# Moving a tile's load and split, and the weights' loads, to later places in the attention stage of a fused attention and two-layer MLP

## The chip, the cores and the metric

The kernel runs on one core of one Trainium2 chip. The metric is the device time of one execution in microseconds; the time before is 1116.73 us, the median of 3 runs (1113.96 to 1124.78).

## The reference

Three parts follow each other. The whole is float32 in and out.

```python
# attention: batch 4, 8 heads, 576 positions, head dimension 64
scores = q @ k.T / 8 + bias          # bias: a small MLP of the relative position, per head
attn = exp(scores - max(scores)); attn = attn / (sum(attn) + 1e-9)
x = (attn @ v) as [2304 tokens, 512]
# layer 0: w_in [512, 2048], w_out [2048, 512]
h = x @ w_in;  x = (h * cos(h)) @ w_out
# layer 1: the same sizes, h = max(h, 0) + alpha * min(h, 0) in the place of h * cos(h)
```

The four weight matrices arrive as 64-bit floats, and are made into 32-bit ones on the chip.

## The kernel before, in words

**Attention** works on 16 pairs n (four pairs of heads, each for four batches; n = 4 * head pair + batch). A pair has five stages s: stages 1 to 4 hold 128 query rows of both heads, stage 0 the last 64 rows of both. A stage is: TensorE computes S (`emit_S`, L457), VectorE adds the bias and takes the maximum (`emit_max`, L473, tile P, or Pr for stage 0), ScalarE takes the exponential in place (`emit_exp`, L486). Then TensorE turns P (L550, L561, into T), ScalarE and VectorE copy that out of PSUM (L535, L537), and TensorE multiplies by v (L572, L575). Each pair's output goes to the DRAM tensor x_d in two pieces, A and B (L593). Pairs 0 to 3 are begun while the bias is still computed; from pair 4 (`FIRST`) on, TensorE's order is fixed, and the order of stages in a pair is 1, 0, 2, 3, 4.

**Weight jobs** run beside the attention, one step at a time (`step`, `bg`). A job `wi(0, f)` prepares one of 16 slabs of layer 0's w_in: SyncE loads the raw 64-bit slab into a tile raw (`load_raw`, two buffers), ScalarE makes two integer parts of it (wc L217 and wp L218, in `conv`), VectorE does two operations on wc (L223, L224), GpSimd adds wp (L227), then splits it into a rounded high and a low part (L306, L310), so that two TensorE products of reduced precision make one of float32. Slabs 6 to 15 are staged in a tile st and stored to w_d (L313). A job `stage_wo(0, k)` for k = 3 to 7 takes two slabs of w_out, raw 2k and 2k + 1, combines them, and splits four groups one after another through the same single-buffered tile st, then named sw: high part on ScalarE (L243), low part on GpSimd (L245), one or two stores to DRAM (L260). The next group's high part has to wait for these stores.

**Layer 0** (`h_phase0`) begins with the first tile of x, the first 512 tokens, which are batch 0: its four pieces xlo0 to xlo3 come from pairs 0, 4, 8 and 12. For each piece `split_x` loads xlo from x_d on SyncE's queue (L185), and splits it: xhi on ScalarE (L768), the low part on GpSimd (L770). These are written late in the program, but a scheduler (with a timeline of its own, and priorities) sets each engine's order, and puts an operation with few conditions early; ScalarE, VectorE, GpSimd and SyncE then take their lists strictly in that order. `behind` adds a condition to the scheduler's order: with its default kind it puts one instruction after another without a wait at run time.

In h_phase0, TensorE computes h (L785), ScalarE, VectorE, ScalarE and VectorE compute h * cos(h) (L793 to L798), and the rest of the weight jobs runs beside it.

Of the kernel before, what the change touches and what calls it, by code (L numbers as in the profile page):

```python
# [9 lines left out]
F32 = mybir.dt.float32  # L10
F32R = mybir.dt.float32r
I32 = mybir.dt.int32
U32 = mybir.dt.uint32
I64 = mybir.dt.int64
AF = mybir.ActivationFunctionType
# [25 lines left out]
FIRST, SIDE, SMOD, BFIRST, BRATE, SPL, WS0, WSR, PER = 4, 6, 2, 8, 2.5, 3, 28, 3.2, 1.0  # L41
# [30 lines left out]
def attn_mlp_kernel(ctx: ExitStack, tc: tile.TileContext, a: dict, out: bass.AP):  # L72
    nc = tc.nc
    ve, se, ge, te, sy = nc.vector, nc.scalar, nc.gpsimd, nc.tensor, nc.sync
# [94 lines left out]
    keep = lambda k, ins: tc.keep_in_program_order(ins) if k < len(KEEP) and KEEP[k] else ins  # L169
# [9 lines left out]
    raws_w = {}  # L179
    pinned = []  # L180
    anchor = []
    last = [None]

    def fetch(out, in_):
# [2 lines left out]
    def behind(ins, prev, kind=mybir.DependencyClass.NoSync):  # L187
        tc.add_manual_dep(ins.ins, prev.ins.name, mybir.DependencyInfo(kind, mybir.DependencyReason.DATA), reason="order")
        return ins

    def later(ins, prev):
        return behind(ins, prev, mybir.DependencyClass.Sync)

    def load_raw(layer, f, part):
        src = (a["wi1"], a["wi2"])[layer][f] if part == 0 else (a["wo1"], a["wo2"])[layer][f * 128:(f + 1) * 128, :]
        nm = f"{layer}_{f}_{part}"
        if wide:
            raw = wpool["s"].tile([128, 512, 2], I32, tag="raw", name=f"raw{nm}")
            ins = fetch(raw.rearrange("p n t -> p (n t)"), src.bitcast(I32))
        else:  # L200
            raw = wpool["s"].tile([128, 512], F32, tag="raw", name=f"raw{nm}")
            ins = fetch(raw, src)
        if anchor:
            behind(ins, anchor[-1])
        raws_w[layer, f, part] = raw

    def conv(layer, f, part, box):
        nm = f"{layer}_{f}_{part}"
        if (layer, f, part) not in raws_w:
            load_raw(layer, f, part)  # L210
            yield
        raw = raws_w.pop((layer, f, part))
        signed = layer == 1 and part == 1
        if wide:
            c = wpool["c"].tile([128, 512], I32, tag="c", name=f"wc{nm}")
            p = wpool["c"].tile([128, 512], I32, tag="p", bufs=1, name=f"wp{nm}")
            se.activation(out=c.bitcast(F32), in_=raw[:, :, 1].bitcast(F32), func=AF.Copy, scale=2.0 ** -112)  # L217
            se.activation(out=p, in_=raw[:, :, 0].bitcast(U32), func=AF.Copy, scale=2.0 ** -29)  # L218
            yield
            if signed:  # L220
                ve.tensor_scalar(c, c, 3, zs[:, f:f + 1].bitcast(I32), op0=ALU.logical_shift_left, op1=ALU.bitwise_xor)
            else:
                ve.tensor_scalar(c, c, 3, None, op0=ALU.logical_shift_left)  # L223
            ve.scalar_tensor_tensor(out=c, in0=raw[:, :, 1], scalar=-2 ** 31, in1=c,  # L224
                                    op0=ALU.bitwise_and, op1=ALU.bitwise_xor)
            yield
            ge.tensor_tensor(out=c, in0=c, in1=p, op=ALU.add)  # L227
            yield
            box.append(c.bitcast(F32))
        else:  # L230
            if signed:
                ve.tensor_scalar(raw, raw, sgn[:, f:f + 1], None, op0=ALU.mult)
                yield
            box.append(raw)
# [83 lines left out]
    bg = []  # L318

    def step(n=1):  # L320
        for _ in range(n):
            if not bg:
                return
            g = bg.pop(0)
            try:
                with tc.high_priority(offset=LP):
                    next(g)
            except StopIteration:
                continue
            bg.insert(0, g)  # L330

    def attention():
        with ExitStack() as c:
# [41 lines left out]
            sums = {}  # L375
# [105 lines left out]
            def emit_exp(n, s, h, e, nm):  # L481
                u, col = place[s, h]
                if (n, u) not in sums:
                    count["m"] += 1
                    sums[n, u] = sume[count["m"] % len(sume)]
                keep(3, se.activation(out=e, in_=e, func=AF.Exp, bias=nm, scale=-1.0,  # L486
                                      accum_out=sums[n, u][:, col, 0:1]))
                Pt[n, s, h] = e


# [179 lines left out]
            ns = 0  # L670
            NS = len(stages)
            i = j = 0
            while i < NS or pend_exp or waiting or fill:
                new = []
                if i < NS:
                    n, u, s = stages[i]
                    if n == FIRST:
                        steady.append(1)
                    hp, b = pairs[n]
                    more_bias(max(BFIRST + int(BRATE * j), GNEED[s]))  # L680
                    for m in range(FIRST, NP):
                        f = pos[m, 1]
                        if i == f - 6:
                            load_qkv(m)
                            splits[m] = split_qk(m)
                        if f - SPL <= i < f:
                            next(splits[m], None)
                    while n not in done:
                        next(side, None)
                    pss = emit_S(n, s)  # L690
                    new = [(n, s, h) + emit_max(n, s, h, ps) for h, ps in enumerate(pss)]
                for x in range(len(pend_exp) if i >= NS else len(pend_exp) + len(new) - ELAG):
                    if not pend_exp:
                        pend_exp, new = new, []
                    emit_exp(*pend_exp.pop(0))
                pend_exp += new
                if i < NS:
                    if b == B - 1 and hp + 1 < NHP:
                        for h in range(len(pss)):
                            load_bias(hp + 1, s + 4 * h)  # L700
                    if ng == NG and ns < len(JOBS) and j >= WS0 + WSR * due:
                        make, args, cost, need = JOBS[ns]
                        if ns == 0:
                            load_raw(*need[0])
                        bg.append(make(*args))
                        if ns + 1 < len(JOBS):
                            load_raw(*JOBS[ns + 1][3][0])
                        due += cost
                        ns += 1
                while waiting and all((waiting[0][0], *k) in Pt for k in place if place[k][0] == waiting[0][1]):  # L710
                    recip(*waiting[0])
                    fill += fillers(*waiting.pop(0))
                m = 2 if s else 1
                credit += PER * (1.85 if s else 1.6)
                if steady:
                    if i >= NS and not pend_exp and not waiting:
                        fill += tails.pop() if tails else []
                    want = {1: (0, 1), 0: (0, 3), 2: (0, 2), 3: (0, 1, 3), 4: (0, 2)}[s] if i < NS else range(4)
                    while fill and fill[0][2] in want:
                        fill.pop(0)[1]()  # L720
                else:
                    while fill and credit > 0:
                        d, fn, _ = fill.pop(0)
                        credit -= d
                        fn()
                    if not fill:
                        credit = min(credit, 0.0)
                wsteps += SR * m
                step(int(wsteps))
                wsteps -= int(wsteps)  # L730
                j += m
                i += 1
# [9 lines left out]
    def h_phase0():  # L742
# [5 lines left out]
        with ExitStack() as c:  # L748
# [7 lines left out]
            def split_x(t, cc):  # L756
                t0, n = TILES[t]
                xp = (wpool["x"], xh_p, xs_p, wpool["x"], xh_p)[t]
                width = 256 if t == 2 else TMAX
                lo = xp.tile([128, width], F32R, tag="xlo", name=f"xlo{t}_{cc}")  # L760
                r = lo.bitcast(F32)
                ins = fetch(r[:, 0:n], x_d[cc, :, t0:t0 + n])
                if anchor:
                    behind(ins, anchor[-1])
                yield
                hi = xp.tile([128, width], F32R, tag="xhi", name=f"xhi{t}_{cc}")
                xt[t, cc] = (hi, lo)
                se.activation(out=hi[:, 0:n], in_=r[:, 0:n], func=AF.Copy)  # L768
                eng = ve if t else ge
                eng.tensor_tensor(out=lo[:, 0:n], in0=r[:, 0:n], in1=hi[:, 0:n].bitcast(F32), op=ALU.subtract)  # L770
                yield
# [447 lines left out]
```

## Time and profile before

| | us |
|---|---|
| median of 3 runs | 1116.73 |
| the profiled execution | 1119.18 |
| its span, first to last instruction | 1117.4 |
| TensorE (PE) busy | 1063.2 |
| VectorE (DVE) busy | 809.9 |
| ScalarE (ACT) busy | 646.0 |
| GpSimd (POOL) busy | 255.0 |

A row of a view names the line, the engine, the operation and the tiles (out<-in). Idle time stands in brackets behind the operation that ended it, with what released it. Matmuls overlap, and their ends are modelled, so the idle time of PE is read more safely than its busy time. The steady attention is read here by pairs: the stretch from one pair's first exponential to the next one's.

### The profile page before, as it was taken

The page shows a single profiled execution, that of the slowest core. Times are in us where ns is not written, and L with a number is a line of the kernel's source. Part 1 is how long each engine was busy: PE and PEld are TensorE (multiplying, and loading weights), DVE is VectorE, ACT ScalarE, POOL GpSimd, SP SyncE. Part 2 cuts the span into 40 slices and gives each one's busy share as a digit, 9 for nine tenths or more (in the row PEclk, how much of TensorE's full clock was granted, in tenths as well). Part 3 has the DMA queues.
Part 4 walks back from the last instruction along what each step waited for, and adds up shares of the span by engine and source line. Part 5 has one row for each costly group of instructions (what it writes and reads, how often), then busy time and mean ns, then how long its engine had stood idle before and what let it go on. Part 6 is the DMA issues. An engine that isn't in the chain of part 4 may idle for free.

```text
span 1117.4 us, 18861 instructions
## 1 busy us (share of the span) xinstructions
PE 1063.2 (95%) x7078; PEld 900.6 (81%) x7078; DVE 809.9 (72%) x1304; ACT 646.0 (58%) x1084; POOL 255.0 (23%) x248
## 2 busy tenths in 40 slices
PE   7689899999799998999899999999999999999998
PEld 2246577777567787988799999998888889999998
DVE  8886687767775789787677777757766747767673
ACT  6897678867775565565344454456555534444442
POOL 5305666655442120000000000312322210000000
PEclk9899999999999999999999999999999999999999
DMA  8666657756449773535657455596666549654621
GB/s 274 215 179 184 200 154 225 231 163 231 158 148 316 266 253 132 161 131 170 216 199 228 149 159 181 201 333 211 215 217 206 199 152 346 209 199 128 212 66 49
DMA packets 107660, 219.77 MB, mean 197 GB/s; under 512 B 11569, under 2 KB 57393, under 8 KB 106161
## 3 DMA queue, kind: packets, MB, share of 16 engines
q1 hardware_dynamic: 77104, 157.74, 44.4%
q10 hardware_dynamic: 28032, 50.34, 12.0%
q0 software_dynamic: 2432, 10.49, 2.4%
q8 instruction: 56, 0.92, 0.4%
q14 instruction: 36, 0.29, 0.1%
HBM read 133.98 MB, written 84.56 MB: 196 GB/s over the span
## 4 chain that ended last, share of the span: by engine, by line
PE 71%; DMA 8%; DVE 6%; ACT 3%; issue 2%; POOL 1%; SPq 0%; ACTq 0%; POOLq 0%; DVEq 0%
PE v L1114 18%; PE ob L983 14%; PE h L785 9%; PE oc L983 9%; PE oa L983 9%; PE S L457 4%; DMA w_d<-sw 3%; PE x_B L575 2%; PE T_B L550 2%; PE T_A L550 1%; DVE tb L794 1%; POOL sw L245 1%; PE x_A L575 1%; DVE tb L795 1%; DVE tb L798 1%
## 5 line engine op out<-in xcount | busy, mean ns | idle before, releaser
L1114 PE MATMUL v<-x,v 128*128 128x512 f32 (+1 forms) x984 | 198.0, 364 | 0.0
L785 PE MATMUL h<-xhi,w 128*128 128x512 f32 (+1 forms) x640 | 186.0, 374 | 7.8 <-DVE tb L798 7.6
L1114 PEld LDWEIGHTS v<-x,v 128*128 128x128 f32 x984 | 168.5, 189 | 29.5
L785 PEld LDWEIGHTS h<-xhi,w 128*128 128x128 f32 x640 | 116.8, 190 | 31.4 <-issue 7.9
L227 POOL TENSOR_TENSOR wc<-wc,wp 128x512 int32<-128x512 int32 x64 | 85.6, 1337 | 208.8 <-DVE wc L224 151.8
L785 PE MATMUL h<-xlo,w 128*128 128x512 f32 (+1 forms) x320 | 119.3, 373 | 0.0
L965 ACT ACTIVATE op<-a 128x768 fp32r<-128x768 f32 x84 | 70.5, 844 | 83.5 <-PE ob L983 27.3
L966 DVE TENSOR_TENSOR op<-a,op 128x768 fp32r<-128x768 f32 x84 | 80.1, 957 | 51.0 <-ACT op L965 50.0
L473 DVE CUSTOM_DVE_ANT_0 P<-S,bt 128x576 f32<-128x576 f32 x128 | 91.5, 750 | 29.1 <-PE S L457 19.3
L486 ACT ACTIVATE P<-P,nm 128x576 f32<-128x576 f32 x128 | 98.5, 772 | 19.3 <-DVE nm L473 19.1
L965 ACT ACTIVATE op<-b 128x768 fp32r<-128x768 f32 x84 | 70.7, 844 | 65.6 <-PE ob L983 23.4
L966 DVE TENSOR_TENSOR op<-b,op 128x768 fp32r<-128x768 f32 x84 | 79.7, 954 | 30.0 <-ACT op L965 29.9
L1125 DVE SCALAR_TENSOR_TENSOR u<-v,asg,u 128x1024 f32<-128x1024 f32 (+2 forms) x48 | 48.0, 1013 | 40.5 <-ACT u L1124 40.1
L983 PE MATMUL ob<-op,wo 128*128 128x384 f32 x432 | 76.4, 336 | 0.0
L983 PEld LDWEIGHTS ob<-op,wo 128*128 128x128 f32 x432 | 75.1, 188 | 0.0
L793 ACT ACTIVATE ta<-h,quart 128x1024 int32<-128x1024 f32 (+1 forms) x40 | 40.9, 1023 | 51.7 <-PE h L785 31.1
L785 PEld LDWEIGHTS h<-xlo,w 128*128 128x128 f32 x320 | 60.8, 190 | 11.0
L457 PE MATMUL S<-kh,qh 64*128 64x288 f32 (+1 forms) x270 | 54.4, 355 | 15.1 <-DVE nm L473 14.2
L1124 ACT ACTIVATE u<-v,sgn 128x1024 f32<-128x1024 f32 (+2 forms) x48 | 43.0, 898 | 40.7 <-PE v L1114 40.6
L794 DVE SCALAR_TENSOR_TENSOR tb<-ta,h 128x1024 f32<-128x1024 int32 (+1 forms) x40 | 44.4, 1109 | 24.5 <-ACT ta L793 24.4
L797 ACT ACTIVATE tb<-tb,hpi 128x1024 f32<-128x1024 f32 (+1 forms) x40 | 42.3, 1059 | 24.6 <-DVE tb L795 17.1
L224 DVE SCALAR_TENSOR_TENSOR wc<-raw,wc 128x512 int32<-128x512 int32 x64 | 54.0, 848 | 1.3
(154 smaller groups left out, 2148.1 us busy)
## 6 DMA issues: line engine op xcount, KB each, us to landing
a<-g_d SPq DMA_DIRECT2D x60, 384.0 KB, 4.5
b<-g_d SPq DMA_DIRECT2D x48, 384.0 KB, 5.0
raw<-in_wi_dram SPq DMA_DIRECT2D x32, 512.0 KB, 3.8
raw<-in_wo_dram SPq DMA_DIRECT2D x32, 512.0 KB, 4.1
g_d<-tb ACTq DMA_DIRECT2D x32, 512.0 KB, 3.4
g_d<-u ACTq DMA_DIRECT2D x28, 512.0 KB, 2.9
bias_d<-be SPq DMA_DIRECT2D x36, 295.5 KB, 3.6
w_d<-sw SPq DMA_DIRECT2D x35, 256.0 KB, 3.1
```

Of the source, the lines that this page charges most:

```text
L224: ve.scalar_tensor_tensor(out=c, in0=raw[:, :, 1], scalar=-2 ** 31, in1=c, op0=ALU.bitwise_and, op1=ALU.bitwise_xor)
L227: ge.tensor_tensor(out=c, in0=c, in1=p, op=ALU.add)
L457: pe(te.matmul(ps[:, hf, 0:HS], lhsT=w[r, 128 * i:128 * i + 128], rhs=m[r, c0:c0 + HS], start=(j == 0), stop=(j == len(terms) - 1)))
L473: keep(2, ve.tensor_tensor_reduce(out=sn.rearrange("p (a b) -> p a b", a=2), in0=ps[:, :, 0:HS], in1=bt[hp, s].rearrange("p (a b) -> p a b ...
L486: keep(3, se.activation(out=e, in_=e, func=AF.Exp, bias=nm, scale=-1.0, accum_out=sums[n, u][:, col, 0:1]))
L785: te.matmul(ps, lhsT=w_[:, wx, w], rhs=xx[:, 0:n], start=(j == 0), stop=(j == 11))
L794: ve.scalar_tensor_tensor(out=g, in0=tt, scalar=-C1, in1=h, op0=ALU.mult, op1=ALU.add)
L965: se.activation(out=o[:, 0], in_=x, func=AF.Copy)
L966: lows.append(ve.tensor_tensor(out=o[:, 1], in0=x, in1=o[:, 0].bitcast(F32), op=ALU.subtract))
L983: ins = te.matmul(ps[:, m], lhsT=x[:, sl] if L else w[:, sl], rhs=w if L else x, start=first, stop=kk == NK - 1 and n == 2, skip_group_che ...
L1114: ins = te.matmul(both[:, i, 0:a1 - a0], lhsT=w[:, wx, 128 * cc:128 * cc + 128], rhs=x[:, xx, cc, a0 - o:a1 - o], start=(n == 0), stop=(n ...
L1125: ve.scalar_tensor_tensor(out=g, in0=ps, scalar=asg[:, f:f + 1], in1=g, op0=ALU.mult, op1=ALU.max)
```

## The change

Four edits, none of which adds or removes an operation; one of SyncE's issues becomes a merged row. (1) The load of the first x tile's piece cc is put behind the first exponential of pair 4cc + 2, and its high part behind the first exponential of pair 4cc + 3. (2) The loads of a job's raw slabs come in the order of their use: a job `stage_wo` first asks for its own second slab, and the next job's first slab is asked for after that. (3) From pair 4 to the end of the attention, raw loads and the two ScalarE parts of `conv` are put behind the exponential that was written last. (4) Exponentials lose their own program-order mark, which was off before (`KEEP` has two entries).

```diff
+    def hold(ins):
+        return behind(ins, exps[-1]) if FIRST in firsts and not pinned else ins
...
         if anchor:
             behind(ins, anchor[-1])
+        hold(ins)
         raws_w[layer, f, part] = raw
...
-            se.activation(out=c.bitcast(F32), in_=raw[:, :, 1].bitcast(F32), func=AF.Copy, scale=2.0 ** -112)
-            se.activation(out=p, in_=raw[:, :, 0].bitcast(U32), func=AF.Copy, scale=2.0 ** -29)
+            hold(se.activation(out=c.bitcast(F32), in_=raw[:, :, 1].bitcast(F32), func=AF.Copy, scale=2.0 ** -112))
+            hold(se.activation(out=p, in_=raw[:, :, 0].bitcast(U32), func=AF.Copy, scale=2.0 ** -29))
...
+    def job(g, more, nxt):
+        for r in more:
+            load_raw(*r)
+        k = 0
+        for _ in g:
+            if nxt and k >= (2 if more else 0):
+                load_raw(*nxt)
+                nxt = None
+            yield
+            k += 1
...
-                keep(3, se.activation(out=e, in_=e, func=AF.Exp, bias=nm, scale=-1.0,
-                                      accum_out=sums[n, u][:, col, 0:1]))
+                exps.append(se.activation(out=e, in_=e, func=AF.Exp, bias=nm, scale=-1.0,
+                                          accum_out=sums[n, u][:, col, 0:1]))
+                firsts.setdefault(n, exps[-1])
...
-                        bg.append(make(*args))
-                        if ns + 1 < len(JOBS):
-                            load_raw(*JOBS[ns + 1][3][0])
+                        bg.append(job(make(*args), need[1:], JOBS[ns + 1][3][0] if ns + 1 < len(JOBS) else None))
...
                 ins = fetch(r[:, 0:n], x_d[cc, :, t0:t0 + n])
-                if anchor:
-                    behind(ins, anchor[-1])
+                behind(ins, anchor[-1] if anchor else firsts[4 * cc + 2])
...
-                se.activation(out=hi[:, 0:n], in_=r[:, 0:n], func=AF.Copy)
+                ins = se.activation(out=hi[:, 0:n], in_=r[:, 0:n], func=AF.Copy)
+                if not t:
+                    behind(ins, firsts[4 * cc + 3])
```

What the scheduler makes of it: TensorE's order is the same row for row. The other four engines differ in the attention and a little in h_phase0. The conv of job f comes up to one job later than before, and has caught up by the time of `raw0_6_1`, w_out's first slab. Piece 0 of x stays where it was on both queues; piece 1's high part moves by a pair, pieces 2 and 3 by a pair each.

ScalarE, around the high part of piece 2 (xhi0_2). Exponentials are P{pair}_{tile} or Pr{pair}, nm{pair}_{column}; T and L are copies out of PSUM. Before:

```order
L486 ACTIVATE P9_3_3186,sume2_118<-P9_3_3186,nm9_4_3187 128x576
L486 ACTIVATE P9_3_3186,sume2_118<-P9_3_3186,nm9_8_3189 128x576
L768 ACTIVATE xhi0_2_4862<-xlo0_2_4852 128x512
L535 ACTIVATE T59_A_3240<-L9_A_3235 128x2x256
L486 ACTIVATE P10_0_3221,sume3_119<-P10_0_3221,nm10_1_3222 128x576
```

After:

```order
L503 ACTIVATE P11_0_3477,sume5_121<-P11_0_3477,nm11_1_3478 128x576
L553 ACTIVATE T10_B_3501<-Tr10_3502 128x8x64
L783 ACTIVATE xhi0_2_4862<-xlo0_2_4852 128x512
L503 ACTIVATE P11_0_3477,sume5_121<-P11_0_3477,nm11_5_3480 128x576
L553 ACTIVATE T10_B_3501<-T10_B_1_3538 128x2x256
```

The high part moves from ahead of pair 10's first exponential to behind pair 11's; its load keeps its place on SyncE's queue.

ScalarE, from the first to the fifth high part of w_out's groups (sw{layer}_{k}_{group}). Before:

```order
L535 ACTIVATE T12_A_3906<-T12_A_3_3929 128x2x256
L243 ACTIVATE sw0_3_0_3202<-wc0_6_1_3042 128x256
L486 ACTIVATE P12_3_3962,sume2_118<-P12_3_3962,nm12_4_3963 128x576
...
L535 ACTIVATE T13_A_4157<-T13_A_3_4180 128x2x256
L243 ACTIVATE sw0_4_0_3517<-wc0_8_1_3343 128x256
L486 ACTIVATE P13_3_4212,sume4_120<-P13_3_4212,nm13_4_4213 128x576
```

After:

```order
L503 ACTIVATE P12_3_3963,sume2_118<-P12_3_3963,nm12_8_3966 128x576
L249 ACTIVATE sw0_3_0_3166<-wc0_6_1_3042 128x256
L553 ACTIVATE T512_A_4024<-L12_A_4019 128x2x256
...
L503 ACTIVATE P14_0_4257,sume5_121<-P14_0_4257,nm14_1_4258 128x576
L249 ACTIVATE sw0_4_0_3461<-wc0_8_1_3343 128x256
L553 ACTIVATE T13_B_4276<-Tr13_4277 128x8x64
```

The group of k = 4 stood one pair behind the group of k = 3; now it stands a pair and two exponentials' places behind it. The group of k = 5 goes from just ahead of pair 15's first exponential to behind its Pr15 and the copy after it.

SyncE's queue, around w_out's raw slabs (raw0_{slab}_1) in pairs 11 and 12. Before:

```order
L593 DMA x_d_58<-xe10_B_3663 128x320
L313 DMA w_d_78<-st14_2911 128x1024
L404 DMA bt3_8_3714<-bias_d_57 128x512
L405 DMA bt3_8_3714<-bias_d_57 128x64
L185 DMA raw0_7_1_3091<-in_wo1_dram 128x1024
L593 DMA x_d_58<-xe11_A_3783 128x256
L313 DMA w_d_78<-st15_3009 128x1024
L593 DMA x_d_58<-xe11_B_3920 128x320
```

After:

```order
L187 DMA raw0_7_1_3040<-in_wo1_dram 128x1024
L611 DMA x_d_58<-xe10_B_3664 128x320
L421 DMA bt3_8_3719<-bias_d_57 128x512
L422 DMA bt3_8_3719<-bias_d_57 128x64
L319 DMA w_d_78<-st14_2909 128x1024
L611 DMA x_d_58<-xe11_A_3787 128x256
L187 DMA raw0_8_1_3091<-in_wo1_dram 128x1024
L611 DMA x_d_58<-xe11_B_3923 128x320
L319 DMA w_d_78<-st15_3007 128x1024
```

Slab 7 is now asked for before slab 8 (which stood earlier on the queue before), and the store of st15 comes behind the store of xe11_B.

## Rows read from the trace of the kernel before

**Rows 1.** The page: busy time, share of the span and instructions of each engine.

```profile
PE 1063.2 (95%) x7078; PEld 900.6 (81%) x7078; DVE 809.9 (72%) x1304; ACT 646.0 (58%) x1084; POOL 255.0 (23%) x248
```

**Rows 2.** Windows of pairs 5 to 14: length, busy by engine, PEclk, DMA share, GB/s.

```profile
151.81:168.91 17.10, 15.74 (x146) 12.24 (x143) 14.80 (x35) 13.60 (x33) 12.36 (x15) 1.00 0.55 159
168.91:184.74 15.83, 15.68 (x143) 12.42 (x144) 11.03 (x30) 13.33 (x32) 10.36 (x11) 1.00 0.59 203
184.74:200.38 15.64, 15.29 (x141) 11.75 (x141) 12.06 (x32) 12.88 (x29) 10.20 (x11) 1.00 0.93 296
200.38:216.19 15.81, 15.81 (x146) 12.25 (x143) 11.32 (x31) 12.38 (x29) 9.90 (x11) 1.00 0.71 227
216.19:234.71 18.52, 15.90 (x144) 12.09 (x142) 13.98 (x35) 13.07 (x30) 11.13 (x14) 1.00 0.59 181
234.71:251.67 16.96, 16.80 (x141) 13.45 (x142) 10.55 (x28) 12.21 (x29) 9.00 (x10) 0.90 0.44 139
251.67:267.08 15.41, 15.41 (x144) 12.10 (x143) 12.64 (x33) 13.04 (x31) 9.12 (x10) 1.00 0.91 289
267.08:285.61 18.53, 16.15 (x146) 12.09 (x144) 14.12 (x38) 14.00 (x33) 8.79 (x11) 1.00 0.44 159
285.61:306.36 20.75, 16.12 (x142) 12.20 (x142) 14.94 (x37) 15.39 (x36) 7.98 (x9) 1.00 0.50 167
306.36:325.32 18.96, 16.87 (x144) 12.43 (x144) 12.10 (x30) 13.84 (x33) 7.54 (x7) 1.00 0.43 131
```

**Rows 3.** Timeline, ScalarE, the high parts of pieces 1 and 2.

```profile
167.90 0.63 ACT L768 ACTIVATE xhi<-xlo 128x512 fp32r<-128x512 f32 x1 [2.21 <-DMA xlo<-x_d]
...
233.70 0.63 ACT L768 ACTIVATE xhi<-xlo 128x512 fp32r<-128x512 f32 x1 [3.44 <-DMA xlo<-x_d]
```

**Rows 4.** Chain that ended last: start, time, the load of piece 2.

```profile
229.53 4.14 DMA xlo<-x_d
```

**Rows 5.** Timeline, TensorE, the first matmul after piece 2's wait.

```profile
234.87 1.22 PE L572 MATMUL x_A<-T_A,v 128*128 128x256 f32 x2 [2.74 <-ACT T_A L535]
```

**Rows 6.** Waits of ScalarE, 267 to 325.4 us: total, times, longest.

```profile
ACT sw L243 <- DMA w_d<-sw: 6.6, 6, 2.2
ACT wp L218 <- DMA raw<-in_wo_dram: 3.9, 2, 2.6
```

**Rows 7.** Timeline, ScalarE, high parts sw0_3_0, sw0_4_0, sw0_5_0.

```profile
280.32 0.42 ACT L243 ACTIVATE sw<-wc 128x256 fp32r<-128x256 f32 x1
...
300.80 0.42 ACT L243 ACTIVATE sw<-wc 128x256 fp32r<-128x256 f32 x1 [0.64 <-DMA w_d<-sw]
...
325.00 0.42 ACT L243 ACTIVATE sw<-wc 128x256 fp32r<-128x256 f32 x1 [0.91 <-DMA w_d<-sw]
```

**Rows 8.** Timeline, ScalarE, the end of pair 8 and the start of pair 9.

```profile
213.68 0.66 ACT L218 ACTIVATE wp<-raw 128x512 int32<-128x512 uint32 x1
214.24 0.77 ACT L486 ACTIVATE P<-P,nm 128x576 f32<-128x576 f32 x1
...
216.19 0.78 ACT L486 ACTIVATE P<-P,nm 128x576 f32<-128x576 f32 x1
...
219.25 0.77 ACT L486 ACTIVATE Pr<-Pr,nm 128x576 f32<-128x576 f32 x1
```

**Rows 9.** Timeline, VectorE, pair 4.

```profile
134.55 0.49 DVE L591 TENSOR_TENSOR xe_B<-x_B,T_B 128x320 f32<-128x320 f32 x1 [3.21 <-PE x_B L572]
...
136.19 1.75 DVE L223 TENSOR_SCALAR wc<-wc 128x512 int32<-128x512 int32 x1
```

**Rows 10.** Timeline, TensorE, pair 4.

```profile
138.66 0.40 PE L457 MATMUL S<-kh,qh 64*128 64x288 f32 x2 [1.18 <-DVE nm L473]
```

**Rows 11.** Timeline, SyncE's queue, the store of xe11_B.

```profile
279.02 0.32 SPq L593 DMA_DIRECT2D x_d<-xe_B  x1
```

**Rows 12.** Line L223 over the whole span: ns minimum, median, maximum.

```profile
L223 DVE TENSOR_SCALAR wc<-wc x48: 414/421/1748, 90.0 to 878.2; 128x512 int32<-128x512 int32 x48
```

**Rows 13.** Windows, a stretch of h_phase0 (columns as in Rows 2).

```profile
440.00:480.00 40.00, 37.66 (x244) 34.53 (x245) 31.51 (x45) 21.27 (x32) 1.29 (x1) 1.00 0.50 158
```

More of the change, by code (lines that the diff above doesn't have):

```diff
@@ L181, in attn_mlp_kernel @@
     anchor = []
+    exps = []
+    firsts = {}
     last = [None]
```

## The prediction

> **What bounds the kernel now.** I read the page's table of engines first: TensorE is busy for 1063.2 of a span of 1117.4 us, the next engine for 809.9 [rows 1]. So the time can fall by no more than what TensorE stands idle, and only where it does. I then cut the steady attention into pairs by windows. The undisturbed pairs are 6, 7, 8 and 11: 15.83, 15.64, 15.81 and 15.41 us, with TensorE busy for nearly all of each [rows 2]. Their mean, 15.67 us, is what a pair costs when nothing is late. Against it, pair 5 (17.10) is 1.43 too long, pair 9 (18.52) 2.85, pair 10 (16.96) 1.29, pair 12 (18.53) 2.86, pair 13 (20.75) 5.08 and pair 14 (18.96) 3.29 [rows 2]. These six excesses, 16.8 us, are the prize; the reader should ask for each what was late.
>
> For that I read the timeline of ScalarE, the chain of waits, and the waits by tile. In pairs 5 and 9 ScalarE stands for 2.21 and 3.44 us at the high part of an x piece, waiting for its load [rows 3]; the load of piece 2 starts at 229.53 and takes 4.14 us [rows 4], and TensorE then has a gap of 2.74 us, since ScalarE's copy of T came after the wait [rows 5]. Pair 10 shows no gap in its window: TensorE is busy for 16.80 of 16.96, but at a granted clock of 0.90 on the average [rows 2], so for part of the stretch at 1.2 in place of 2.4 GHz, just after that gap. I put its 1.29 down to the same wait. In pairs 12 to 14 ScalarE waits for w_out: 6.6 us in six waits for the stores of the group before, which leave the one tile sw, and 3.9 us in two waits for a raw slab [rows 6].
>
> **The change, part by part.** No operation is added or removed, and `behind` makes no wait at run time. What is priced is thus each instruction's new place on the queue of its engine, since each takes its list strictly in order.
>
> *The x pieces.* Piece 1's high part goes from ahead of pair 6 to between pair 7's two first exponentials, piece 2's from ahead of pair 10 to pair 11, piece 3's from ahead of pair 14 to pair 15; their loads keep their places on SyncE's queue, so there are some 15 us more between the two, against a load of 4.14 us [rows 4]. The waits go: −1.4 (pair 5), −2.85 (pair 9), −1.3 (pair 10). The high part itself (0.63 us on ScalarE [rows 3]) is still done.
>
> *Pair 4.* VectorE's 1.75 us on wc stands ahead of pair 4's maximum, and TensorE waits for that maximum for 1.18 us [rows 9, 10]. After the change wc of an earlier job stands ahead of xe_B, where VectorE waits for TensorE for 3.21 us anyhow [rows 9], and nothing of it is left ahead of that maximum: −1.2.
>
> *The raw slabs.* Slab 7 is asked for ahead of slab 8, in the order of use. The longest wait for a raw slab, 2.6 us, is that of slab 7; it and the other one (3.9 together) [rows 6] lie within the excess of pairs 12 to 14, so they are not counted by themselves.
>
> *The ring through sw.* From sw0_3_0 at 280.32 to sw0_4_0 at 300.80 are 20.48 us, and to sw0_5_0 at 325.00 another 24.2 [rows 7]. Four groups, each a high part, a low part and a store, pass through one tile in that time. The places on ScalarE's list offer exactly one pair for the first of these, 15.67 us; the ring needs more, and ScalarE stands for the difference. After the change sw0_4_0 comes a pair and two exponentials' places later. In pair 8 and 9 the distances between the exponentials are 216.19 − 214.24 = 1.95 and 219.25 − 216.19 = 3.06 us [rows 8]. So the step from k = 3 to k = 4 gets 15.67 + 1.95 = 17.6 us, the one from 4 to 5, behind Pr and a copy, about 15.67 + 3.06 + 0.6 = 19.3. Against 20.48 the ring still lacks 2.9 and 1.2, together 4.1 us. Of the 11.2 us of excess in pairs 12 to 14 (2.86 + 5.08 + 3.29), 4.1 stays and 7.1 goes: −7.1. This holds the raw slab in order and piece 3's high part too.
>
> The parts that go make 1.2 + 1.4 + 2.85 + 1.3 + 7.1 = 13.85 us.
>
> *What the new places cost.* The two integer parts of conv (0.66 us each [rows 8]) now stand behind an exponential. For jobs 2, 3 and 5 both stand between two exponentials of one stage (1.3 us), and four single operations, high parts of x among them, do so too (0.65). If each delays a stage in full this is 3 × 1.3 + 4 × 0.65 = 6.5 us. Below stands nothing, since one such operation stood between two exponentials in pair 8 (213.68, ahead of the exponential at 214.24 [rows 8]), and that pair took an undisturbed 15.81 us [rows 2]. On SyncE's queue the store of st15 now stands behind the store of xe11_B, which was issued at 279.02 [rows 11]; sw0_3_0, at 280.32 [rows 7], uses the same tile and has to wait for it. If that store takes as long as the load of piece 2 (4.14), sw0_3_0 can start at 279.02 + 4.14 = 283.2 at the earliest, some 3 us later; the part of this that a stage's slack doesn't take up lies between 0 and 3, and I estimate 1. Together 0 to 8 (rounded down from 9.5, since a delay of 6.5 asks that no stage has any slack, against pair 8); I take 3, nearer to zero, because the only such row of before showed no cost.
>
> Sum: −13.85 + 3 = −10.85 us. The profiled execution took 1119.18, 2.45 more than the median of 1116.73; the rows are its rows, and I take the difference off the median: **1105.9, so 1106 us**.
>
> *Does it come through to the end?* After pair 15 the tail of the weight jobs and layer 0 follow, whose order hardly differs. From 440 to 480 us TensorE is busy for 37.66 of 40 [rows 13]: it is the bound, with little slack to give a gain back. The weight jobs have caught up by w_out's first slab, so nothing of the attention's work is pushed behind its end. I let the gain stand.
>
> *A rule on the two vector engines.* GpSimd and VectorE work on the same tiles when wp and wc pass between them. VectorE's L223 takes 414, 421 and 1748 ns at the least, the median and the most of 48 [rows 12]: nearly all are short, and one as long cost pair 4 its 1.18. The Trainium skill, "GPSIMD Engine Reference", section 1, says that GpSimd's SBUF interfaces are shared with VectorE, with contention in a 2-port mode or with two SBUF inputs; by that a moved operation can lose, as well as win, its clear field. The median of 421 says that this is rare here; what it would give is the third rival below.
>
> **The rivals.** *First: layer 0 takes part of it back.* The raw loads, x pieces and slabs come at other moments, and in h_phase0 the worst window of 40 us I looked at has 40 − 37.66 = 2.34 us of idle TensorE [rows 13]. If the shift makes as much again in two windows, 4.7 us are lost: 1110.6. For it: x pieces and conv compete with VectorE and ScalarE there. Against: that order is nearly the same.
>
> *Second: the change doesn't do what it says in pairs 12 to 14.* The ring's 20.48 us [rows 7] were measured with ScalarE waiting in it; if its own length grows with the distance, since low parts and stores wait for others, the stall stays. Then the gain is 1.2 + 1.4 + 2.85 + 1.3 − 3 = 3.75: 1113.0.
>
> *Third, slower: GpSimd in VectorE's way.* Of 14 slabs the L223 operation stands in another place, and one that runs beside GpSimd takes 1.748 in place of 0.421 [rows 12], 1.33 more. If each of them delays a maximum, and so TensorE, that is 14 × 1.33 = 18.6: 1105.9 + 18.6 = 1124.5. From nine of the 14 on (10.85 / 1.33 = 8.2) it is slower than before. Against: the median, and GpSimd is busy for 255 of 1117 us only [rows 1].
>
> *Fourth: better.* Nothing of the new places costs, and the ring is covered in full: 1.2 + 1.4 + 2.85 + 1.3 + 11.2 = 17.95, 1098.8.
>
> **How the numbers follow.** Forecast 0.53, first rival 0.15, second 0.13, third 0.06, fourth 0.13. A change of 1% (11.2 us) is about what a measurement of this kernel can tell from none, since the three runs before lie 10.8 us apart. Below 1105.6 (faster) lie the fourth rival and about half of the forecast, whose own range by the new waits (0 to 8) is 1102.9 to 1110.9: 0.13 + 0.27 = 0.40. Above 1127.9 only the third rival with further delays, and what I have overlooked: 0.04. Within 1%: 0.56. The range goes from 1098 (fourth) to 1115 (second, with 2 us for the medians' own spread); outside lie the third and something of the fourth and the second.
>
> **What would show it right or wrong.** In windows of pairs in the new profile, 5, 9 and 10 should last about 15.7 us, pair 10 at a granted clock of 1.00; ScalarE's timeline should show no wait for a load of x. TensorE's gap in pair 4 should be gone. Waits for raw slabs should be gone, and those for sw's stores down from 6.6 to about 4 us, with pairs 12 to 14 nearer to 17 than to 19 us. New would be ScalarE at sw0_3_0 waiting for the store of st15. I am wrong if pairs that were undisturbed (6 to 8, 11) grow by a microsecond each, if L223's median rises, or if TensorE's idle time in h_phase0 rises by what the attention gained.

## The result, and the profile after

The changed kernel took 1107.70 us (median of 6 runs, 1104.60 to 1110.60) against 1118.78 for the kernel before, now timed 6 times too. The ratio on record is 0.9908, 95% interval 0.9878 to 0.9937 (such a ratio need not be the quotient of the medians). Timed a second time, beside other kernels on another occasion, it gave 0.9935 (0.9914 to 0.9955). It is faster by 0.6 to 0.9%; 1106 was forecast. The profiled execution's span is 1105.9 us, 11.5 less than before.

The page, busy time by engine: nothing was added or removed, and TensorE works as long as before [rows 1].

```profile
PE 1063.1 (96%) x7078; PEld 899.6 (81%) x7078; DVE 810.3 (73%) x1304; ACT 645.9 (58%) x1084; POOL 248.5 (22%) x248
```

Windows of pairs 5 to 15 after the change (columns as in [rows 2]: length, busy by engine, PEclk, DMA share, GB/s).

```profile
148.52:164.57 16.05, 15.49 (x145) 12.19 (x143) 13.01 (x33) 13.14 (x32) 10.27 (x12) 1.00 0.34 116
164.57:179.99 15.42, 15.42 (x145) 12.17 (x143) 13.07 (x33) 13.09 (x32) 9.64 (x12) 1.00 0.62 205
179.99:197.89 17.90, 16.76 (x148) 12.58 (x145) 11.10 (x31) 13.26 (x32) 11.57 (x13) 1.00 0.92 302
197.89:213.54 15.65, 15.00 (x140) 11.75 (x140) 13.40 (x33) 12.48 (x30) 9.50 (x11) 1.00 0.59 192
213.54:229.30 15.76, 15.76 (x145) 12.18 (x143) 11.11 (x31) 12.95 (x31) 11.54 (x12) 1.00 0.53 178
229.30:244.95 15.65, 15.57 (x143) 12.05 (x142) 12.76 (x33) 12.60 (x30) 8.00 (x11) 1.00 0.63 207
244.95:262.28 17.33, 16.75 (x147) 12.50 (x145) 11.04 (x31) 13.27 (x32) 11.78 (x13) 1.00 0.92 295
262.28:278.49 16.21, 15.56 (x144) 12.17 (x143) 14.17 (x36) 13.35 (x32) 8.98 (x9) 1.00 0.39 131
278.49:295.09 16.60, 15.72 (x144) 12.00 (x142) 13.19 (x34) 14.30 (x33) 6.54 (x8) 1.00 0.50 177
295.09:313.06 17.97, 15.55 (x141) 11.70 (x140) 13.48 (x36) 14.62 (x33) 6.91 (x8) 1.00 0.52 167
313.06:329.91 16.85, 15.72 (x136) 12.05 (x134) 12.93 (x31) 14.56 (x34) 8.61 (x8) 1.00 0.61 190
```

Against [rows 2], pairs 5, 9 and 10 are short now (−1.05, −2.76 and −1.31), and pair 10 runs at a granted clock of 1.00. Pairs 12, 13 and 14 lost 2.32, 4.15 and 0.99. Pairs 7 and 11 are the new long ones, +2.26 and +1.92. Pair 15, counted to its last exponential's end, grew too: before it was this window, 14.46 us.

```profile
325.32:339.78 14.46, 13.61 (x123) 10.34 (x124) 11.12 (x31) 12.86 (x32) 6.00 (x7) 1.00 0.53 185
```

From pair 4's first exponential to the last one, 209.1 us became 202.2 (−6.9). What lies ahead of pair 4 was 2.9 us shorter, and what follows the last exponential 1.7 (777.6 to 775.9).

These stretches are cut at ScalarE's exponentials, and an exponential can move against TensorE's rows. TensorE's order is the same before and after, so its own rows can be compared one by one. Here are pair 15's first row and layer 0's first product, before and then after:

```profile
325.61 0.37 PE L457 MATMUL S<-kh,qh 128*128 128x288 f32 x1 [0.77 <-DVE sm_B L495]
...
339.95 0.48 PE L785 MATMUL h<-xhi,w 128*128 128x512 f32 x1
```

```profile
313.61 0.44 PE L474 MATMUL S<-kh,qh 128*128 128x288 f32 x1
...
328.76 0.48 PE L802 MATMUL h<-xhi,w 128*128 128x512 f32 x1
```

On these rows pair 15 grew by 0.8 us (14.34 to 15.15) and not by 2.39: of its longer window TensorE is busy for 2.11 more (15.72 against 13.61), since it is already in layer 0 when the last exponential ends. Layer 0 begins 11.2 us earlier, and what follows is 0.4 us shorter and not 1.7.

What ScalarE did at the former waits, from its timeline after the change: the high parts of pieces 1 and 2, which wait for nothing now [rows 3], and the first groups of w_out's pairs 3, 4 and 5 [rows 7].

```profile
181.22 0.63 ACT L783 ACTIVATE xhi<-xlo 128x512 fp32r<-128x512 f32 x1
...
246.19 0.63 ACT L783 ACTIVATE xhi<-xlo 128x512 fp32r<-128x512 f32 x1
...
276.24 0.40 ACT L249 ACTIVATE sw<-wc 128x256 fp32r<-128x256 f32 x1
...
295.87 0.40 ACT L249 ACTIVATE sw<-wc 128x256 fp32r<-128x256 f32 x1
...
317.85 0.42 ACT L249 ACTIVATE sw<-wc 128x256 fp32r<-128x256 f32 x1
```

The steps of the ring are 19.63 and 21.98 us. ScalarE's waits in pairs 12 to 14, as [rows 6]: 1.9 us for sw's stores, and none for a raw slab. wp now waits for GpSimd's sum; before, it waited there once, 1.4 us, with GpSimd at a low part of sw.

```profile
ACT sw L249 <- DMA w_d<-sw: 1.9, 2, 1.2
...
ACT wp L224 <- POOL wc L233: 1.2, 2, 1.0
```

Much of the wait for sw's stores was put off rather than removed: pair 15, which had none, has 2.1 us of it (0.72 and 1.43), and ScalarE's total over the whole program, before and after, is this.

```profile
ACT sw L243 <- DMA w_d<-sw: 14.2, 11, 2.6
...
ACT sw L249 <- DMA w_d<-sw: 13.4, 8, 4.0
```

The wait of wp for GpSimd also makes pair 7 long. Timelines of ScalarE, GpSimd and TensorE there, in this order:

```profile
195.35 0.69 ACT L224 ACTIVATE wp<-raw 128x512 int32<-128x512 uint32 x1 [2.00 <-POOL wc L233]
```

```profile
193.47 0.62 POOL L312 CAST st<-wc 128x512 fp32r<-128x512 f32 x1 [6.10 <-DMA w_d<-st]
194.05 1.27 POOL L233 TENSOR_TENSOR wc<-wc,wp 128x512 int32<-128x512 int32 x1
```

```profile
196.84 0.33 PE L568 MATMUL T_B<-ident,P 128*128 128x128 f32 x1 [0.98 <-ACT P L503]
```

Read from below: TensorE waits for pair 7's last exponential. It stands on ScalarE's list behind wp of slab 10. wp has one tile, so it must wait until GpSimd has added the wp before (L233). GpSimd's list had stood for 6.10 us at the staging tile st, whose store took 6.7 us from issue to landing, in a pair with a DMA share of 0.92: pairs 7 and 11 load the bias of the next head pair.

### The profile page after: what moved, and what is told of

Read it like the earlier page. It is cut to its first block, busy times and chain, and to the rows that moved or that the text cites. A ratio compares the mean times of both kernels' runs of the same rounds, so it can differ in the third digit from the quotient of the medians.

```text
span 1105.9 us, 18859 instructions
## 1 busy us (share of the span) xinstructions
PE 1063.1 (96%) x7078; PEld 899.6 (81%) x7078; DVE 810.3 (73%) x1304; ACT 645.9 (58%) x1084; POOL 248.5 (22%) x248
## 4 chain that ended last, share of the span: by engine, by line
PE 74%; DMA 6%; DVE 5%; ACT 3%; POOL 2%; issue 2%; SPq 1%; ACTq 0%; POOLq 0%; DVEq 0%
PE v L1131 18%; PE ob L1000 14%; PE h L802 10%; PE oc L1000 9%; PE oa L1000 9%; PE S L474 4%; PE x_B L593 2%; DMA w_d<-sw 2%; PE T_B L568 2%; PE T_A L568 1%; PE x_A L593 1%; DVE tb L812 1%; DVE tb L811 1%; DMA w_d<-st 1%; POOL sw L251 1%
## 5 line engine op out<-in xcount | busy, mean ns | idle before, releaser
L233 POOL TENSOR_TENSOR wc<-wc,wp 128x512 int32<-128x512 int32 x64 | 85.8, 1341 | 207.2 <-DVE wc L230 135.7
L135 DVE TENSOR_SCALAR u<-at,thr 128x576 f32<-128x576 f32 (+17 forms) x120 | 53.0, 511 | 2.3 <-PE bps L140 2.3
L224 ACT ACTIVATE wp<-raw 128x512 int32<-128x512 uint32 x64 | 42.8, 669 | 20.1 <-POOL wc L233 13.9
```

The source lines that it names most:

```text
L135: ve.tensor_scalar(u[:, 0:n], at[:, 0:n], thr[:, m:m + 1], None, op0=ALU.max)
```

## Experiments

Ratios are against the kernel before, with their 95% intervals. The code shown is cut, and is set against the changed kernel except where another is named. Edit (4) is in every run but the kernel before; edit (3) alone was not run. Of pairs I give the windows of the profiled execution. The stretch ahead of pair 4, where the orders hardly differ, began the attention's steady part anywhere from 127.4 to 135.7 us, so spans of single profiles are not compared.

### Edit (1) alone

```diff
     def hold(ins):
-        return behind(ins, exps[-1]) if FIRST in firsts and not pinned else ins
+        return ins
...
-                        bg.append(job(make(*args), need[1:], JOBS[ns + 1][3][0] if ns + 1 < len(JOBS) else None))
+                        bg.append(make(*args))
+                        if ns + 1 < len(JOBS):
+                            load_raw(*JOBS[ns + 1][3][0])
```

> Edit (1) alone: the x pieces' loads and high parts behind later exponentials; no hold, old order of raw loads. My theory (each excess of a pair has its own cause): pairs 5, 9 and 10 lose 1.1, 2.8 and 1.3 us, as in the changed kernel; w_out's groups still stand one pair apart on ScalarE, so pairs 12 to 14 together stay within 2 us of 58.2; span about 5.2 us shorter, ratio 0.995. Rival (the new places of conv are what clears pairs 5, 9 and 10 too): those pairs stay at 17.1, 18.5 and 17.0, ratio 0.999 to 1.001.

Measured: 1.0100 (1.0065 to 1.0136), slower; the medians are 1126.06 and 1118.37. The theory fell. In the attention the waits for x's loads were gone, pairs 5 and 10 fell to 15.98 and 16.26 and pairs 12 to 14 stayed at 57.3, but pair 9 kept 18.64, and pairs 7, 11 and 15 grew to 16.57, 16.74 and 17.47. So the causes of the excesses are not independent: with the new places the scheduler dealt the conv operations anew, and some landed badly. Pair 9 shows how. VectorE, then GpSimd, then TensorE:

```profile
213.75 1.08 DVE L229 TENSOR_SCALAR wc<-wc 128x512 int32<-128x512 int32 x1
...
215.68 1.74 DVE L230 SCALAR_TENSOR_TENSOR wc<-raw,wc 128x512 int32<-128x512 int32 x1
217.34 0.74 DVE L490 CUSTOM_DVE_ANT_0 Pr<-S,bt 128x576 f32<-128x576 f32 x1
```

```profile
215.33 1.55 POOL L457 TENSOR_TENSOR kl<-rk,kh 128x640 fp32r<-128x640 f32 x1
```

```profile
218.15 0.40 PE L474 MATMUL S<-kh,qh 64*128 64x288 f32 x2 [1.84 <-DVE nm L490]
```

The operation on wc (L230) takes 0.69 us at the median. Here it runs beside GpSimd, takes 1.74, stands ahead of pair 9's maximum, and TensorE has a gap of 1.84 us: the prediction's third rival, met in a part of the change and not in the whole. Pair 9 explains a gain that did not come, and not why the run is slower than before. On TensorE's rows the steady attention is no longer than before: pair 4 began 1.5 us earlier, and layer 0's first product 1.4 earlier (339.95 before). The program ended 3.3 later, so 4.7 us were lost in layer 0. TensorE, with its longest gap there, and ScalarE ahead of it:

```profile
338.51 0.48 PE L804 MATMUL h<-xhi,w 128*128 128x512 f32 x1
...
412.43 0.47 PE L804 MATMUL h<-xhi,w 128*128 128x512 f32 x1 [3.01 <-DVE tb L817]
```

```profile
403.23 0.42 ACT L785 ACTIVATE xhi<-xlo 128x256 fp32r<-128x256 f32 x1 [3.32 <-DMA xlo<-x_d]
```

ScalarE stands for 3.32 and then 2.08 us for loads of x's next tile, VectorE behind it for the high parts, and TensorE for VectorE's tb: the wait for x taken out of the attention is met again in layer 0, as the first rival has it. Other waits make up the rest of the 4.7. The profile is of one of the shortest of six runs (1122.1 to 1132.3), and what makes the others longer stays open.

### Edits (2) and (3) alone

The x pieces' two `behind` lines are taken out again, the rest is the changed kernel.

> Edits (2) and (3) alone: raw loads in the order of use, and conv held behind exponentials; x pieces in their old places. My theory: pairs 12 to 14 come to about 51 us together (58.2 before), pair 4 loses its gap; pairs 5, 9 and 10 keep 17.1, 18.5 and 17.0; pair 11 keeps the changed kernel's new wait of wp (its first slab stands between two exponentials again), pair 7 does not, as its wp no longer stands there; ratio 0.994 to 0.996. Rival (the hold is what gives all): 0.991, as the whole change.

Measured: 0.9960 (0.9932 to 0.9987). Pairs 12 to 14 came to 52.3 us, pairs 5, 9 and 10 stayed long, at 17.02, 19.68 and 17.08, pair 11 had the wait of wp (18.26), and pair 7 had not (15.45). My theory holds here, but for pair 9, of which 18.5 was expected. Pair 10's window shows the clock again:

```profile
213.69:233.37 19.68, 15.35 (x140) 11.77 (x140) 12.74 (x33) 13.37 (x31) 11.29 (x14) 1.00 0.51 160
233.37:250.45 17.08, 16.93 (x141) 13.72 (x142) 11.95 (x30) 12.67 (x30) 8.66 (x10) 0.90 0.54 175
```

With the wait for piece 2 back in pair 9, pair 10 is back at 0.90. The two alone make +1.0% and −0.4%, together −0.6 to −0.9%: without the hold edit (1) costs. That it pays with it, by 0.2 to 0.5%, is a difference of estimates whose intervals overlap.

### Edit (2) alone, and all but edit (2)

For edit (2) alone `hold` returns its instruction as it is, and the x pieces' lines are out.

> Edit (2) alone: raw slabs asked for in the order of use. My theory: ScalarE's waits for raw slabs in pairs 12 to 14 go (3.9 us), but the ring through the one tile sw sets these pairs, and waits for its stores grow by as much: 0 to -1 us, ratio 0.999 to 1.000. Rival (the slab asked for too late is the cause of pairs 12 to 14): -4 us or more, ratio 0.996 or less.

Measured: 1.0001 (0.9978 to 1.0023). Without the hold, no wait for a raw slab is left in pairs 12 to 14, and those for sw rise from 6.6 to 8.6 us: the next thing in the chain was late, as expected. It took back only a part: in the profile the three pairs came from 58.2 to 55.4 us. No such gain shows in the times, whose interval reaches 2.5 us either way.

For all but edit (2) the `job` line is the old one again.

> Edits (1) and (3), raw loads in the old order. My theory: the order of the raw loads is worth nothing here either: within 2 us of the changed kernel, ratio 0.990 to 0.993. Rival (with the hold, slab 7 behind slab 8 comes too late): ScalarE waits 2 us or more for a raw slab in pairs 12 to 14, ratio 0.994 or more.

Measured: 0.9943 (0.9921 to 0.9964). The rival's wait was there: with the hold, the slab asked for too late costs 2.6 us in pair 13, which is 18.50 long (16.60 in the changed kernel).

```profile
ACT wp L224 <- DMA raw<-in_wo_dram: 2.6, 1, 2.6
```

So in the profiles edit (2) shortens pairs 12 to 14 by 2.8 us without the hold, and pair 13 by 1.9 with it. That it is worth more with the hold is not shown, nor does a gain show in the times: this interval overlaps both of the changed kernel's.

### VectorE's part of the hold, on edit (1)

Here the code is set against edit (1) alone; w1 is the operation on wc just ahead.

```diff
-            ve.scalar_tensor_tensor(out=c, in0=raw[:, :, 1], ...)
+            w2 = ve.scalar_tensor_tensor(out=c, in0=raw[:, :, 1], ...)
+            if layer == 0 and FIRST in firsts and not anchor:
+                behind(w1, maxes[-1])
+                behind(w2, maxes[-1])
```

> Edit (1), and of edit (3) only a hold of VectorE's two operations of conv, behind the maximum written last; raw loads and ScalarE's parts are not held. In the run of edit (1) alone, pair 9 kept 18.6 us, since VectorE's second operation on wc took 1.74 us beside GpSimd and stood ahead of pair 9's maximum. My theory: that operation now stands behind the maximum, pair 9 comes to 16.5 or less; pairs 12 to 14, where ScalarE's list is as before, stay at 56 us or more; ratio 0.996 to 1.003. Rival (pair 9 is long for another reason, such as a late store or load): pair 9 stays above 18.

Measured: 1.0050 (1.0024 to 1.0077), beyond my bounds. Pair 9 fell from 18.64 to 16.25, so what held it was the slow operation ahead of the maximum. Pairs 12 to 14 stayed long (58.8). Layer 0 lost time as in edit (1) alone: ScalarE waited there for loads of x for 3.37 and 1.71 us, and TensorE had a gap of 2.69. A timed gain over edit (1) alone is not shown; the intervals overlap.

### An own tile for the first groups

```diff
-        st = wpool["t"].tile([128, 2, 2, 256], F32R, tag="st", ...)
+        if g == 0 and "g0" in wpool:
+            st = wpool["g0"].tile([128, 1, 2, 256], F32R, tag="g0", ...)
+        else:
+            st = wpool["t"].tile([128, 2, 2, 256], F32R, tag="st", ...)
```

> The changed kernel with an own tile (2 KB a partition) for the first of the four groups of each pair of w_out slabs, so that three steps and not four share the tile sw. My theory: ScalarE's waits for sw's stores fall from 9.5 us to 3 or less, and pairs 12 to 15, 67.6 us in the changed kernel against 62.7 undisturbed, lose 3 us: ratio to the kernel before 0.988. Rival (these waits lie beside other work, or ScalarE waits for GpSimd in their place): no shorter than the changed kernel, 0.991.

Measured: 1.0027 (1.0000 to 1.0053). The theory fell. Pair 14 took 21.05 us (17.97 in the changed kernel). On ScalarE's list wp's wait for GpSimd, 1.51 us, and sw's for a store, 1.21, now stand one behind the other, and TensorE has one gap of 3.23 us where it had 1.5; behind that gap its granted clock was lower, 0.92 over the pair against 1.00. The window, then TensorE:

```profile
294.61:315.66 21.05, 17.40 (x144) 13.41 (x142) 14.39 (x37) 15.37 (x35) 7.93 (x8) 0.92 0.49 165
```

```profile
306.94 0.93 PE L593 MATMUL x_B<-T_B,v 128*128 128x320 f32 x2 [3.23 <-ACT T_B L556]
```

And layer 0 began with a gap of 9.87 us. TensorE, then ScalarE:

```profile
364.46 0.80 PE L807 MATMUL h<-xhi,w 128*128 128x512 f32 x1 [9.87 <-DVE tb L820]
```

```profile
359.06 0.63 ACT L249 ACTIVATE sw<-wc 128x512 fp32r<-128x512 f32 x1 [11.46 <-DMA w_d<-sw]
```

The last group of k = 6 waits for the store of the group before, issued behind seven loads of slabs and up to 8.6 us on its way, and layer 0's functions stand behind that group on ScalarE's list.

With the own tile for k = 3 to 5 only (`g == 0 and k < 6`):

> The kernel with an own tile for the first group, but for w_out's pairs 3 to 5 only; the last two use the common tile as in the changed kernel. My theory: the 9.9 us gap in TensorE at the start of layer 0 came from a store of the sixth pair behind ten loads of slabs on SyncE's queue, and is gone; pair 14 stays near 21 us, since wp there waits for GpSimd; ratio 0.993 to 0.996. Rival (the gap belongs to the own tile as such): it stays at 8 us or more, ratio 1.00.

Measured: 0.9960 (0.9935 to 0.9984). The gap is gone, and pair 14 stays long, at 21.70 us with a granted clock of 0.84.

### A second tile for wp

```diff
+            turn2[0] ^= 1
+            if turn2[0] and "p2" in wpool:
+                p = wpool["p2"].tile([128, 512], I32, tag="p2", name=f"wp{nm}")
+            else:
...
```

> The changed kernel with a second tile for wp (2 KB a partition, every other conv): ScalarE can write the next wp while GpSimd still needs the last. My theory: the waits of wp for GpSimd's sum (2.0, 1.4 and 1.0 us in pairs 7, 11 and 14) go, pairs 7 and 11 come from 17.9 and 17.3 to below 16.2, the attention loses 3 us, ratio to the kernel before 0.988. Rival (the wait moves to the next thing that GpSimd holds, the staging tile, or layer 0 takes it back): pairs 7 and 11 shorter, but ratio 0.991 or more.

Measured: 1.0007 (0.9983 to 1.0032). Both theories fell in part: pairs 7 and 11 grew, to 18.37 and 19.04. With a tile free, the scheduler put the next job's wp at the end of pair 7, where its own slab had not landed:

```profile
199.85 0.67 ACT L229 ACTIVATE wp<-raw 128x512 int32<-128x512 uint32 x1 [3.20 <-DMA raw<-in_wi_dram]
```

So a free buffer did not help where the list filled it at once. A second staging tile st, which might loosen both rings, was not tried.

### Moving two or three rows

A `behind` that names a later exponential, given when that one is written, moves single rows. First the changed kernel once more, for comparison.

> The changed kernel once more, beside the two that follow, since x_hold and the others were timed against it only through the kernel before. Both theories: ratio 0.989 to 0.994.

Measured: 0.9935 (0.9914 to 0.9955), 1108.40 us.

```diff
+                if (n, s, h) in PUSH:
+                    behind(wps[PUSH[n, s, h]], exps[-1])
```

With `PUSH` for wp of slab 10 behind pair 7's last exponential, and of w_out's first slab behind pair 11's:

> The changed kernel with two rows of ScalarE's list moved by one exponential: wp of slab 10 behind pair 7's last exponential, wp of w_out's first slab behind pair 11's last. My theory: wp there waits for GpSimd's sum, and the last exponential waits behind it; after the move that exponential runs 2.0 and 1.4 us earlier, but ScalarE's copy of T behind wp still waits for a part: pairs 7 and 11, 17.9 and 17.3 us, come to 16.0 to 16.8; ratio to the kernel before 0.988 to 0.991. Rival (what is late there is not ScalarE but the bias loads of the next head pair, which come in pairs 7 and 11): both pairs stay above 17.

Measured: 0.9910 (0.9890 to 0.9930), 1106.12 us. Pairs 7 and 11 came to 16.24 and 15.82.

With both behind the first exponentials of pairs 8 and 12, and wp of w_out's slab 11 behind the first exponential of pair 14's stage 3:

> The same two rows moved further, behind the first exponentials of pairs 8 and 12, where GpSimd's sum is done, and wp of w_out's slab 11 moved from ahead of pair 14's exponential 3 to behind it. My theory: pairs 7 and 11 come to 15.7 to 16.2, pairs 8 and 12 grow by 0.3 or less, pair 14 loses its gap of 1.5 us: 4 to 5 us less than the changed kernel, ratio to the kernel before 0.986. Rival (the sum that comes later makes GpSimd late, and the waits come back within the next pair): pairs 8 and 12 grow by what 7 and 11 gain, ratio 0.991.

Measured: 0.9884 (0.9862 to 0.9907), 1103.80 us, the best of all; its interval lies below that of the changed kernel beside it, 0.9914 to 0.9955. Windows of pairs 7, 8, 11, 12 and 14:

```profile
180.02:195.70 15.68, 15.68 (x145) 12.20 (x143) 11.54 (x31) 12.57 (x30) 10.29 (x11) 1.00 0.94 306
195.70:211.82 16.12, 15.48 (x144) 12.14 (x143) 13.81 (x33) 13.05 (x31) 11.14 (x13) 1.00 0.64 221
243.23:258.91 15.68, 15.68 (x144) 12.14 (x143) 11.49 (x31) 12.69 (x30) 10.44 (x11) 1.00 0.92 297
258.91:276.29 17.38, 16.10 (x148) 12.58 (x146) 15.33 (x36) 13.99 (x34) 11.51 (x12) 1.00 0.43 151
292.94:310.57 17.63, 15.95 (x141) 11.53 (x140) 13.35 (x36) 14.63 (x34) 6.91 (x8) 1.00 0.54 170
```

Pairs 7 and 11 are undisturbed at the same DMA share as before: the place of wp was the cause, the bias loads only made it late. The windows of pairs 8 and 12 grew by 0.47 and 1.17, more than the 0.3 expected. In both pairs wp now stands with wc between two exponentials; in pair 12 the two operations that VectorE does on wc meet GpSimd and are long, a maximum comes late, and TensorE has a gap of 1.28 us. That is the third rival again. VectorE, then TensorE:

```profile
261.45 1.77 DVE L231 TENSOR_SCALAR wc<-wc 128x512 int32<-128x512 int32 x1
...
263.74 1.44 DVE L232 SCALAR_TENSOR_TENSOR wc<-raw,wc 128x512 int32<-128x512 int32 x1
```

```profile
266.68 0.40 PE L476 MATMUL S<-kh,qh 64*128 64x288 f32 x2 [1.28 <-DVE nm L492]
```

Pair 14 was to lose 1.5 and lost 0.34.

## Why the prediction was right, and where not

- **What bounds the kernel: right.** TensorE's busy time is the same, and the gain lies where TensorE stood idle.
- **The x pieces: right in size, but not on its own.** −1.4, −2.85 and −1.3 were forecast, −1.05, −2.76 and −1.31 measured, and the run with the pieces in their old places has all three excesses back. But they were summed as if they stood alone, and alone the edit makes the kernel slower: in its profile the time is lost in layer 0, where ScalarE waits for x again.
- **Pair 4: wrong.** Of −1.2 only −0.35 came (21.12 to 20.77). The gap ahead of the maximum is gone, but TensorE then waited 1.8 us for ScalarE's T_B, since wc and wp now stand between pair 4's exponentials.
- **The raw slabs and the ring: right for these pairs.** A list that offers steps of 17.6 and 19.3 was forecast, against the ring's 20.48, with 4.1 us left waiting; measured were steps of 19.63 and 21.98, stalls included, and 1.9 us of waits for sw. The three pairs gave 7.46, against 7.1. That a wait could be put off into pair 15 and behind the attention was not considered.
- **What the new places cost: the step that was mis-sized.** 3 us were taken, of 0 to 8; pairs 7 and 11 grew by 2.26 and 1.92, and pair 15, on TensorE's rows, by 0.8, together 5.0. In pairs 7 and 11 the 0.66 us of an operation were priced, not what it waits for: wp's single tile, and through GpSimd's list the staging tile. Pair 15 has eight operations of conv, sw and xhi on ScalarE where it had five, and 2.1 us of waits for sw, so part of the gain of pairs 12 to 14 was work put off; most of it TensorE did not wait for. The wait of sw0_3_0 for the store of st15 did not come: it stands behind pair 12's last exponential, past the store's landing.
- **Through to the end: right.** On TensorE's rows what follows the attention was not longer, but 0.4 us shorter.
- **The sum: in part luck.** Of the 11.5 us between the two profiles 2.9 lie ahead of pair 4, where the forecast had nothing. From there to layer 0 the change gave 8.3, against 10.85 forecast: what the new places cost beyond 3 us, and what pair 4 did not give, was made good ahead of pair 4. In the second profile of the same kernel pair 4 began at 129.74 and not at 127.75, so most of the 2.9 is not the change's, and the second timing's ratio, 0.9935, is 7 us.

Of the rivals, the second is refuted (pairs 12 to 14), and so is the first for the whole change, though edit (1) alone shows it. The fourth did not come, since the new places cost. The third did not happen in the whole change, where L229 took 412, 422 and 1511 ns at the least, the median and the most (compare [rows 12]), but it did in pair 9 of edit (1) alone and in pair 12 of the last run.

## What to carry to other kernels

Where a scheduler deals fixed lists, an edit's worth is not a sum of removed stalls: look at the places that every list gets, and price each moved operation by what it waits for, not by its duration alone. Count the gain on the rows of the engine that bounds the kernel: here its order was fixed, and windows cut at another engine's rows put 1.3 us into the wrong stretch. Then move single rows: two or three of them gave more here than a second buffer, which only let the scheduler fill the room with something that was late elsewhere.

## What the hardware showed

VectorE's SCALAR_TENSOR_TENSOR on wc takes 0.69 us at the median. In the steady attention of six kernels (before, after, edit (1), edits (2) and (3), edit (2), VectorE's hold) it began 20 times while GpSimd was in a TENSOR_TENSOR, and each time it ended 0.54 or 0.55 us after that one did: 1.09 us where 0.54 was left, 1.33 where 0.79, 1.74 where 1.19. So it ends as if it did most of its work only after GpSimd's operation. The Trainium skill, "SBUF — State Buffer", section "Who interferes with whom", says that the pair of ports that the two share is an exclusive lock, and that a VectorE instruction with two inputs in SBUF contends with a GpSimd instruction that reads SBUF. The trace agrees: this operation reads raw and wc, and the GpSimd operations are ones that read two tiles.
